# Unit 0's distance bias of two score groups moved into PSUM by TensorE, with a new order of the attention steps

## The chip, the core and the metric

The kernel runs on one core of a Trainium2 chip. The metric is device time in microseconds of one launch. Engines are named as in the profile: PE (TensorE, matmuls; PEld its weight loads), DVE (VectorE), ACT (ScalarE), POOL (GpSimd), SP (SyncE, which here only issues DMAs).

## The reference

Local attention with a few global keys, and behind it a mixture of experts whose tokens are dealt out evenly. Batch 4, 8 heads, 768 positions, head size 64, everything float32 at the interface:

```python
scores = scale * np.matmul(q, k.transpose(0, 1, 3, 2))
rel = pos[:, None] - pos[None, :]
is_global = pos[None, :] < int(n_global)                 # n_global = 8
is_local = (rel >= 0) & (rel < int(n_local))             # n_local = 96
keep = is_global | is_local
dist = np.where(is_global & ~is_local, float(n_local), np.abs(rel))
scores = scores + (-slopes[:, None, None] * dist)        # slopes[h] = 2 ** -(h + 1)
scores = np.where(keep, scores, -1e9)
a = np.exp(scores - max); a = a / (sum + 1e-9)
x = (a @ v) as rows of 512 = 8 heads x 64                # 3072 tokens
logits = x @ w_gate; each expert takes 384 tokens in order of the logits
out[mask] = np.maximum(x[mask] @ w1[e], 0) @ w2[e]       # 8 experts, 512 -> 1024 -> 512
```

## The kernel before

**Three stages.** The attention fills about the first 116 us, the routing goes to about 149 us, and the experts (matmuls in bf16) to the end.

**How the attention is tiled.** There are 8 units, 0 to 7; a unit is half a batch, four heads. A unit has two head pairs n = 2u and 2u+1, which the step names call a and b. Only keys near the diagonal and the 8 global keys count, so the positions are cut into 7 key tiles of 120, each against 216 queries. The 7 tiles form three score groups, 0 (tiles 0, 1), 1 (tiles 2, 3) and 2 (tiles 4 to 6). Each group fills 432 columns of one PSUM bank for each of the four heads: four banks in all, `ps0` (two banks, pair a) and `ps1` (two banks, pair b). Group 1 of unit 0 alone is put into four other banks, `po0`, `po1`, `t0`, `t1`, which the attention uses later for other things.

**The steps of a unit.** `KT` and `QT` (DVE, L291) transpose the raw keys and queries in blocks; `KB` and `KP` (ACT, L299), `KS` (POOL, L305 and L306) bring the keys into the tiles' layout; `QO` and `QP` (L318; ACT, for some steps of units 0 and 1 POOL or DVE) do so for the queries. A number behind the letters is the half of a head's 64 channels (0 or 1); for unit 0 the first part of a copy has a step of its own (`KP`, `QP`). Then, for each group g:

- `S0`, `S1`, `S2` (PE, L350): the scores of the group for all four heads, float32.
- `BIga`, `BIgb` (DVE, L368): reads the scores from PSUM and the distances `Dm` from SBUF, writes scores − 8·slope·distance to the tile `P` in SBUF. Two instructions a step, one a head. When both pairs are done the `ps` banks are free for the next group.
- `EXga`, `EXgb` (ACT, L375): exponential of `P` in place, with the factor 1/8.

Then `AV0` and `AV1` (PE, L408) multiply `P` by the values, `OT` (ACT, L415) brings the result out of PSUM, `M0` and `M1` (POOL, L384 to L391) add up the overlapping tiles, `SU` (PE, L425 and L429) makes the sums and the gate's logits, `LT` (DVE, L465), `GT` (POOL), `TK` and `TO` (PE and DVE, L507 and L526) finish the rows. `C0` to `C17` build constants, `WT` starts loads of expert weights.

**What sets the order.** One list of step names, `ORDER`, is written out by hand, and the program is issued in it; each engine takes its own steps in that order and waits at each for what it needs. Ahead of the list stand the loads of units 0 and 1, 64 matmuls on a constant that nothing reads (`warm`, L583), and the building of `Dm` on POOL (L228 to L245). One step, `FW` (L605), is 15 float32 matmuls, 30 passes on PE, whose result nothing reads; it stands between `S2:0` and `S0:1`.

Of the kernel before, what the change touches and what calls it, by code (L numbers as in the profile page):

```python
# [9 lines left out]
FP32 = mybir.dt.float32  # L10
# [21 lines left out]
NT = 7  # L32
QW = 216
# [11 lines left out]
def kernel(  # L45
# [25 lines left out]
    nc.vector.tensor_copy(out=ident_bf, in_=ident)  # L71
# [62 lines left out]
    @later  # L134
    def _():
        nc.gpsimd.memset(tri_bf, 1.0 / 128.0)
        nc.gpsimd.affine_select(out=tri_bf, in_=tri_bf, compare_op=ALU.is_ge, fill=0.0,
                                base=-1, pattern=[[1, 128]], channel_multiplier=-1)
# [83 lines left out]
    with ExitStack() as actx:  # L222
# [23 lines left out]

        natp = actx.enter_context(tc.tile_pool(name="natp", bufs=1))
# [88 lines left out]
        def scores(u, g, spare=False):  # L336
            kA, qTt = kAs[u % 2], qTs[u]
            if spare:
                ps = [ps_o.tile([128, 512], FP32, tag=f"po{i}", name=f"psx{i}_{u}") for i in range(2)]
                ps += [ps_t.tile([128, 512], FP32, tag=f"t{i - 2}", name=f"psx{i}_{u}") for i in (2, 3)]  # L340
                at = lambda a: ps[a]
            else:
                ps = [ps_s.tile([128, 2, 512], FP32, tag=f"ps{w_}", name=f"ps{w_}_{u}_{g}") for w_ in range(2)]
                at = lambda a: ps[a // 2][:, a % 2, :]
            for i in GROUPS[g]:
                _, o, w = POS[i]
                for gd in range(2):
                    for a in range(4):
# [3 lines left out]
                                         start=(gd == 0), stop=(gd == 1), skip_group_check=True)  # L352
# [20 lines left out]
        def expo(n, g):  # L373
            P = Ps[n][:, 2 * g : 2 * g + 2].rearrange("p i t w -> p (i t w)")
            nc.scalar.activation(P, P, AF.Exp, scale=0.125)  # L375

# [162 lines left out]
        def consts_(*which):  # L539
# [767 lines left out]
```

## Time and profile before

| | |
|---|---|
| time, median of 3 runs | 247.12 us (247.04 to 247.24) |
| profiled execution, its own time | 245.83 us |
| span of its records | 244.0 us |
| PE busy | 230.1 us (94%) |
| DVE busy | 145.1 us (59%) |
| ACT busy | 154.1 us (63%) |
| POOL busy | 158.2 us (65%) |

The busy shares are of the whole span, which has three stages of different kind. The page's 40 slices and the table by stretch below say more: in the attention all four engines are busy most of the time, in the experts PE alone. The times of rows are microseconds from the start of the span. The time of a row of merged instructions is from the start of the first to the end of the last.

### The profile page before, as it was taken

What the parts mean: (1) busy time and instruction counts of PE and PEld (TensorE: products, weight loads), DVE (VectorE), ACT (ScalarE), POOL (GpSimd) and SP (SyncE); (2) the same over time, 40 slices, a digit from 0 to 9 for tenths busy, and PEclk for the clock granted to TensorE, in tenths of its full rate; (3) what the DMA queues carried; (4) which work ended last, traced back from release to release, by engine and by line L of the source; (5) the groups of instructions that cost most, each with busy time, mean ns of one, the idle gap of its engine ahead of it and who ended that gap; (6) DMA issues with size and microseconds to landing.
All of it is one profiled execution on the core that took longest, in us unless ns stands there. A gap on an engine that the chain in (4) does not pass through costs nothing.

```text
span 244.0 us, 6976 instructions
## 1 busy us (share of the span) xinstructions
PE 230.1 (94%) x2769; PEld 166.8 (68%) x2769; DVE 145.1 (59%) x323; ACT 154.1 (63%) x298; POOL 158.2 (65%) x290
## 2 busy tenths in 40 slices
PE   8899999999999999999778888999999999999990
PEld 7888888787878788787667746755555565655540
DVE  2998999999999886746887881332051423131220
ACT  2788999999999989744789942423425060524420
POOL 6456977899998999989220017785178685761322
PEclk9999999999999999999999999999999999999998
DMA  6998999699963899999999334999999999999412
GB/s 254 345 368 147 270 377 212 189 293 185 246 125 72 156 203 182 204 166 181 217 212 251 132 131 84 197 168 184 280 257 162 264 209 241 251 149 294 139 48 93
DMA packets 51545, 49.65 MB, mean 203 GB/s; under 512 B 31024, under 2 KB 43056, under 8 KB 51504
## 3 DMA queue, kind: packets, MB, share of 16 engines
q0 software_dynamic: 15728, 26.22, 53.2%
q1 hardware_dynamic: 35776, 22.89, 36.0%
q8 instruction: 24, 0.39, 0.7%
q14 instruction: 17, 0.14, 0.2%
HBM read 56.05 MB, written 9.44 MB: 268 GB/s over the span
## 4 chain that ended last, share of the span: by engine, by line
PE 82%; DVE 7%; ACT 4%; DMA 3%; issue 1%; POOLq 0%; POOL 0%; DVEq 0%; ACTq 0%
PE po L1229 16%; PE po L408 16%; PE ps L350 16%; PE ph L1188 15%; PE t L425 5%; ACT x L522 4%; PE t L429 2%; DVE arena L291 2%; PE ph L1177 2%; PE pxe L1140 2%; DMA w_early<-in_k_dram 2%; PE psx L605 1%; PE pw L507 1%; DMA xe<-x_tok,idi 1%; PE t L507 1%
## 5 line engine op out<-in xcount | busy, mean ns | idle before, releaser
L1191 ACT ACTIVATE hT<-ph 128x384 bf16<-128x384 f32 x56 | 27.5, 491 | 47.5 <-PE ph L1188 46.9
L368 DVE SCALAR_TENSOR_TENSOR P<-Dm,ps 128x432 f32<-128x432 f32 x92 | 49.4, 598 | 12.1 <-PE ps L350 12.1
L375 ACT ACTIVATE P<-P 128x864 f32<-128x864 f32 x48 | 42.5, 928 | 4.6 <-DVE P L368 4.3
L408 PE MATMUL po<-P,v 128*64 128x216 f32 (+6 forms) x576 | 40.5, 293 | 0.0
L408 PEld LDWEIGHTS po<-P,v 128*64 128x64 f32 x576 | 34.1, 137 | 8.9 <-issue 3.1
L387 POOL TENSOR_TENSOR S<-P 128x576 f32<-128x576 f32 (+1 forms) x32 | 38.8, 1214 | 1.7 <-ACT P L375 1.6
L1098 POOL DMA_INDIRECT xe<-x_tok,idi x24 | 24.5, 1020 | 13.1 <-PE ph L1188 7.0
L291 DVE STREAM_TRANSPOSE arena<-w_early 128x768 f32<-128x768 f32 x32 | 29.6, 955 | 3.5 <-DMA w_early<-in_k_dram 3.5
L1229 PEld LDWEIGHTS <-hT 128*128 128x128 bf16 x192 | 18.3, 98 | 19.3
L299 ACT COPY kA<-arena 128x720 f32<-128x720 f32 (+2 forms) x18 | 24.0, 1348 | 5.5 <-DVE arena L291 5.5
L522 ACT ACTIVATE x<-pw,ri 128x64 bf16<-128x64 f32 x112 | 24.4, 346 | 2.8 <-PE pw L507 2.8
L1107 POOL DMA_INDIRECT out_dram<-w_early,ido x15 | 14.9, 994 | 14.7 <-DVE w_early L1232 8.7
L1232 DVE COPY w_early<-po 128x512 f32<-128x512 f32 x15 | 10.4, 691 | 20.3 <-PE po L1229 20.3
L350 PE MATMUL ps<-arena,kA 32*128 32x216 f32 (+2 forms) x416 | 20.9, 333 | 1.0 <-DVE arena L318 0.6
L350 PE MATMUL ps<-qT,kA 32*128 32x216 f32 (+2 forms) x448 | 21.9, 334 | 0.0
L1148 DVE COPY xT<-pxe 128x512 bf16<-128x512 bf16 x18 | 7.0, 417 | 21.9 <-PE pxe L1140 21.9
L415 ACT COPY oT<-po 128x384 f32<-128x384 f32 x32 | 15.1, 479 | 7.3 <-PE po L408 7.3
L350 PEld LDWEIGHTS ps<-qT,kA 32*128 32x128 f32 x448 | 18.7, 185 | 1.1 <-issue 0.3
L350 PEld LDWEIGHTS ps<-arena,kA 32*128 32x128 f32 x416 | 17.6, 185 | 2.7 <-POOL arena L318 1.1
L1229 PE MATMUL po<-w_late,hT 128*128 128x512 bf16 x72 | 16.5, 379 | 0.0
L1188 PE MATMUL ph<-xT,w_late 128*128 128x384 bf16 x96 | 16.1, 326 | 0.0
L1188 PEld LDWEIGHTS <-w_late 128*128 128x128 bf16 x96 | 9.4, 98 | 6.5
(199 smaller groups left out, 381.3 us busy)
## 6 DMA issues: line engine op xcount, KB each, us to landing
w_early<-in_k_dram SPq DMA_DIRECT2D x8, 768.0 KB
w_early<-in_q_dram SPq DMA_DIRECT2D x8, 768.0 KB
v<-in_v_dram SPq DMA_DIRECT2D x32, 180.0 KB
w_late<-in_moe_w_dram POOLq DMA_DIRECT2D x5, 1024.0 KB, 12.8
w_early<-in_moe_w_dram POOLq DMA_DIRECT2D x8, 512.0 KB, 9.0
w_last<-in_moe_w_dram POOLq DMA_DIRECT2D x4, 1024.0 KB, 11.2
arena<-in_moe_w_dram POOLq DMA_DIRECT2D x2, 1024.0 KB, 11.8
x_tok<-x SPq DMA_DIRECT2D x2, 768.0 KB
```

Source lines behind the costliest of these rows:

```text
L291: nc.vector.transpose(out=t, in_=raws[kind, u][:, :, 32 * g : 32 * g + 32])
L299: nc.scalar.copy(out=kAs[u % 2][:, g, i0:i1, 8:128].rearrange("p i (c j) -> p i c j", j=NJ), in_=t[:, i0 * NC5 : i1 * NC5, :].rearrange("p ...
L350: nc.tensor.matmul(at(a)[:, o : o + w], lhsT=kA[r, gd, i, :], rhs=qTt[r, gd, KT * i : KT * i + w], start=(gd == 0), stop=(gd == 1), skip_g ...
L368: nc.vector.scalar_tensor_tensor(out=Ps[n][:, 2 * g : 2 * g + 2, t, :], in0=W, scalar=-8.0 * slopes[2 * (n % NPAIR) + t], in1=st[:, 0 : 2 ...
L375: nc.scalar.activation(P, P, AF.Exp, scale=0.125)
L387: nc.gpsimd.tensor_tensor(out=to[:, :, :, 0:OV], in0=P[:, i0 : i0 + m, :, 0:OV], in1=P[:, i0 - 1 : i0 + m - 1, :, KT:QW], op=ALU.add)
L408: nc.tensor.matmul(po[n, bank][64 * t : 64 * t + 64, a - QB * bank : z - QB * bank], lhsT=v7[:, t, i, :], rhs=Ps[n][:, min(i, 5), t, a - q ...
L522: nc.scalar.activation(x[:, 2 * hf + i, 128 * jj + 64 * t : 128 * jj + 64 * t + 64], ps[:, i, 64 * t : 64 * t + 64], AF.Identity, scale=ri ...
L1098: tc.keep_in_program_order(nc.gpsimd.indirect_dma_start(out=xes[s], out_offset=None, in_=x_tok[:, :], in_offset=bass.IndirectOffsetOnAxis( ...
L1188: nc.tensor.matmul(ph, lhsT=w1_of(e)[:, kc, 128 * fc : 128 * fc + 128], rhs=xT_of[e][:, kc, :, :].rearrange("p t n -> p (t n)"), start=(kc ...
L1191: nc.scalar.activation(hT[:, fc, :], ph, AF.Relu)
L1229: pin(e, nc.tensor.matmul(po, lhsT=hT[:, t, fc, :] if e == 0 else hT[:, fc, 128 * t : 128 * t + 128], rhs=w2_of(e)[:, fc, :], start=(fc == ...
```

## The change

- The distances of two groups are also kept in bf16 (`Db`, an ACT copy of `Dm`), and four diagonal matrices `sid` with −8·slope on the diagonal are made (four DVE instructions). All these numbers are exact in bf16.
- New steps `PB1:0` and `PB0:0`: four bf16 matmuls each, `sid` times `Db`, 432 columns into each head's bank. The scores of groups 0 and 1 of unit 0 are then added on top of that. `BI0` and `BI1` of unit 0 (four steps, eight DVE instructions) fall away.
- The exponential of those groups reads PSUM and writes `P`: for group 0 one ACT instruction a pair, for group 1, whose heads lie in separate banks, two.
- `FW` is gone, and `warm` has 48 matmuls instead of 64.
- The copies of the queries of units 0 and 1 change engine: `QO0:0` and `QO0:1` from POOL to DVE, `QO1:0` from POOL to ACT, `QO1:1` from ACT to DVE, `QP0:0` from ACT to DVE, `QP1:0` from DVE to ACT.
- The cast of `ident_bf` goes from DVE at the start to POOL, in the constant step `C6`.
- The list `ORDER` is new for all units.

```diff
-    nc.vector.tensor_copy(out=ident_bf, in_=ident)
...
+        nc.gpsimd.tensor_copy(out=ident_bf, in_=ident)
         nc.gpsimd.memset(tri_bf, 1.0 / 128.0)
...
+        Db = wmp.tile([128, WB - W0A], BF16)
+        sid = wmp.tile([128, 4, 128], BF16)
+
+        def distances_bf():
+            for h in range(4):
+                nc.vector.tensor_scalar(out=sid[:, h, :], in0=ident, scalar1=-8.0 * slopes[h], scalar2=None, op0=ALU.mult)
+            nc.scalar.copy(out=Db, in_=Dm[:, W0A : WB])
...
+        biased = {}
+
+        def distance_bias(u, g):
+            ps, at = biased[u, g] = score_banks(u, g)
+            lo = (W0A, WA, WA)[g]
+            D = Db[:, WA:WB].rearrange("p (o w) -> p o w", o=1).to_broadcast([128, 2, QW]) if g == 1 else Db[:, lo : lo + 2 * QW]
+            for a in range(4):
+                nc.tensor.matmul(at(a)[:, 0 : 2 * QW], lhsT=sid[:, 4 * (u % 2) + a, :], rhs=D, start=True, stop=False, skip_group_check=True)
...
-                                         start=(gd == 0), stop=(gd == 1), skip_group_check=True)
+                                         start=(gd == 0 and (u, g) not in biased), stop=(gd == 1), skip_group_check=True)
...
         def expo(n, g):
+            u, w_ = divmod(n, 2)
+            if (u, g) in biased:
+                if g == 0:
+                    Ps[n] = pp.tile([128, NT - 1, 2, QW], FP32, tag="P", name=f"P{n}")
+                to = Ps[n][:, 2 * g : 2 * g + 2]
+                ps = pss[u, g]
+                if len(ps) == 4:
+                    for t in range(2):
+                        nc.scalar.activation(to[:, :, t, :], ps[2 * w_ + t][:, 0 : 2 * QW].rearrange("p (i w) -> p i w", w=QW),
+                                             AF.Exp, scale=0.125)
+                else:
+                    nc.scalar.activation(to.rearrange("p i t w -> p t i w"),
+                                         ps[w_][:, :, 0 : 2 * QW].rearrange("p t (i w) -> p t i w", w=QW), AF.Exp, scale=0.125)
+                return
...
-            "KT0:0 KT1:0 KB0:0 QT0:0 KP1:0 QT1:0 KP0:0 KS0:0 KS1:0 QP1:0 KT0:1 QP0:0 QO0:0 S0:0 KB1:0 QO1:0 KB0:1 "
+            "KT0:0 KB0:0 KS0:0 PB1:0 KT1:0 QT1:0 C12:0 KS1:0 PB0:0 QT0:0 KP1:0 QP0:0 KP0:0 QP1:0 KT1:1 KB1:0 "
...
-        QCOPY = {"QO0:0": nc.gpsimd.tensor_copy, "QO1:0": nc.gpsimd.tensor_copy, "QO0:1": nc.gpsimd.tensor_copy}
+        QCOPY = {"QO0:0": nc.vector.tensor_copy, "QO0:1": nc.vector.tensor_copy, "QO1:1": nc.vector.tensor_copy, "QP0:0": nc.vector.tensor_copy}
...
-            elif op == "FW":
-                for m in range(15):
-                    nc.tensor.matmul(pss[0, 1][2][:, 432:512], lhsT=ident, rhs=ident[:, 0:80],
-                                     start=True, stop=True, skip_group_check=True)
...
-            warm(64)
+            warm(48)
             distances()
+            distances_bf()
```

How instructions stand on DVE before, from the first transposes to unit 1's group 0 (`P_315` and `P_319` are the `P` tiles of pairs a and b of unit 0, `psx` the four other banks):

```order
L291 STREAM_TRANSPOSE arena<-w_early 128x768 x4
L71 CAST ident_bf<-ident 128x128
L318 COPY arena<-arena 128x336
L291 STREAM_TRANSPOSE arena<-w_early 128x768 x2
L368 SCALAR_TENSOR_TENSOR P_315<-Dm,ps_0_0_267 128x2x216 x2
L368 SCALAR_TENSOR_TENSOR P_319<-Dm,ps_0_0_268 128x2x216 x2
L291 STREAM_TRANSPOSE arena<-w_early 128x768 x2
L368 SCALAR_TENSOR_TENSOR P_319<-Dm,ps_0_2_332 128x2x216 x2
L368 SCALAR_TENSOR_TENSOR P_315<-Dm,ps_0_2_331 128x2x216 x2
L368 SCALAR_TENSOR_TENSOR P_315<-Dm,psx_0_293 128x2x216
L368 SCALAR_TENSOR_TENSOR P_315<-Dm,psx_0_294 128x2x216
```

The same place on DVE now (lines are those of the new text: L299 is the transpose, L326 the query copy, L387 the bias; here `P_319` is pair a):

```order
L299 STREAM_TRANSPOSE arena<-w_early 128x768 x4
L326 COPY arena<-arena 128x336
L299 STREAM_TRANSPOSE arena<-w_early 128x768
L326 COPY arena<-arena 128x432
L299 STREAM_TRANSPOSE arena<-w_early 128x768 x3
L326 COPY qT_331<-arena 128x768 x2
L387 SCALAR_TENSOR_TENSOR P_319<-Dm,ps_0_2_338 128x2x216 x2
L387 SCALAR_TENSOR_TENSOR P_315<-Dm,ps_0_2_339 128x2x216 x2
L299 STREAM_TRANSPOSE arena<-w_early 128x768 x2
L387 SCALAR_TENSOR_TENSOR P_425<-Dm,ps_1_0_385 128x2x216 x2
L387 SCALAR_TENSOR_TENSOR P_428<-Dm,ps_1_0_384 128x2x216 x2
```

Eight bias instructions of unit 0 are gone, four query copies stand there instead of one, and both transposes of unit 2 that follow stand ahead of unit 1's first bias.

On ACT before, from the first key copy to the first copy out of the values' product:

```order
L299 COPY kA_135<-arena 128x4x120
L299 COPY kA_135<-arena 128x2x120 x2
L318 COPY arena<-arena 128x336
L299 COPY kA_135<-arena 128x4x120
L299 COPY kA_136<-arena 128x6x120 x2
L375 ACTIVATE P_315<-P_315 128x864
L318 COPY qT_375<-arena 128x768
L375 ACTIVATE P_319<-P_319 128x864
L375 ACTIVATE P_315<-P_315 128x864 x2
L299 COPY kA_135<-arena 128x6x120
L415 COPY oT_447<-po_0_410 128x2x6x32
```

And now, without the two exponentials of the last pair's group 1 and what follows them (L307 is the key copy, L404 and L401 the exponential out of PSUM, L408 the one in place):

```order
L307 COPY kA_136<-arena 128x4x120
L307 COPY kA_136<-arena 128x2x120 x2
L326 COPY arena<-arena 128x336
L307 COPY kA_136<-arena 128x4x120
L326 COPY arena<-arena 128x432
L404 ACTIVATE P_315<-ps_0_0_255 128x2x2x216
L404 ACTIVATE P_319<-ps_0_0_254 128x2x2x216
L307 COPY kA_137<-arena 128x6x120
L401 ACTIVATE P_319<-psx_0_239 128x2x216
L401 ACTIVATE P_319<-psx_0_240 128x2x216
L307 COPY kA_137<-arena 128x6x120
L408 ACTIVATE P_319<-P_319 128x864
```

The two exponentials of group 0 stand ahead of both key copies of unit 1, and the 768-wide query copy is gone from here.

On PE before, behind unit 0's group 2 (`po_0` is the values' product of pair a):

```order
L350 MATMUL ps_0_2_332<-arena,kA_135 128x48 x2
L605 MATMUL psx_0_295<-ident 128x80 x15
L350 MATMUL ps_1_0_390<-qT_375,kA_136 128x216 x2
L350 MATMUL ps_1_0_391<-qT_375,kA_136 128x216 x2
```

And now (L369 the scores, L441 the values' product):

```order
L369 MATMUL ps_0_2_339<-arena,kA_136 128x48 x2
L441 MATMUL po_0_367<-P_319,v_0_138 64x216 x4
L441 MATMUL po_0_367<-P_319,v_0_138 64x144 x2
L441 MATMUL po_0_367<-P_319,v_0_138 64x24 x2
L369 MATMUL ps_1_0_384<-qT_331,kA_137 128x216 x2
L369 MATMUL ps_1_0_385<-qT_331,kA_137 128x216 x2
```

Where the 15 unread matmuls stood, pair a's first values' product now stands.

## Rows read from the trace of the kernel before

**Rows 1.** By stretch: us, busy (x instructions) by engine, granted clock, DMA share, GB/s
```profile
9.30:16.30 7.00, 5.98 (x114) 5.09 (x113) 6.65 (x9) 5.61 (x5) 2.12 (x6) 1.00 1.07 316
21.50:83.00 61.50, 61.47 (x1140) 51.22 (x1140) 58.12 (x107) 59.92 (x70) 55.95 (x127) 1.00 0.84 207
83.00:116.00 33.00, 32.73 (x588) 26.44 (x588) 22.50 (x50) 23.10 (x31) 30.99 (x61) 1.00 1.13 188
149.40:236.50 87.10, 87.10 (x560) 49.79 (x561) 23.20 (x46) 31.45 (x63) 51.62 (x53) 1.00 0.94 200
```

**Rows 2.** Chain that ended last, 14 to 30 us: start, us, engine, tile, line
```profile
14.35 1.95 PE ps L350 x38
16.30 3.50 PE psx L605 x30
19.80 1.67 PE ps L350 x32
21.48 2.44 PE po L408 x36
23.92 1.67 PE ps L350 x32
25.59 0.79 PE t L425 x16
...
26.70 1.21 PE po L408 x16
27.91 1.96 PE ps L350 x44
```

**Rows 3.** Timeline, 5 to 24 us: start, us, engine, line, operation, shapes, count
```profile
5.31 3.68 DVE L291 STREAM_TRANSPOSE arena<-w_early 128x768 f32<-128x768 f32 x4 [3.50 <-DMA w_early<-in_k_dram]
6.32 2.08 ACT L299 COPY kA<-arena 128x480 f32<-128x480 f32 x3 [4.23 <-DVE arena L291]
8.19 1.93 POOL L318 COPY arena<-arena 128x432 f32<-128x432 f32 x2 [0.49 <-DVE arena L291]
8.29 0.80 ACT L318 COPY arena<-arena 128x336 f32<-128x336 f32 x1
9.17 1.26 DVE L318 COPY arena<-arena 128x336 f32<-128x336 f32 x1
9.30 0.65 PE L350 MATMUL ps<-arena,kA 32*128 32x216 f32 x8
10.35 1.82 DVE L291 STREAM_TRANSPOSE arena<-w_early 128x768 f32<-128x768 f32 x2
16.34 2.15 DVE L368 SCALAR_TENSOR_TENSOR P<-Dm,ps 128x432 f32<-128x432 f32 x4 [0.39 <-PE ps L350]
20.49 1.48 ACT L299 COPY kA<-arena 128x720 f32<-128x720 f32 x1
21.51 2.15 DVE L368 SCALAR_TENSOR_TENSOR P<-Dm,ps 128x432 f32<-128x432 f32 x4 [1.11 <-PE ps L350]
```

**Rows 4.** Timeline around 61 us, DVE and POOL
```profile
61.12 1.42 POOL L387 TENSOR_TENSOR S<-P 128x576 f32<-128x576 f32 x1
61.39 1.29 DVE L142 TENSOR_SCALAR w_early<-w_early 128x192 int32<-128x192 int32 x1
```

**Rows 5.** Groups with shapes kept apart, 0 to 117 us: busy us, mean ns
```profile
L375 ACT ACTIVATE P<-P 128x864 f32<-128x864 f32 x48 | 42.5, 928 | 4.6 <-DVE P L368 4.3
L415 ACT COPY oT<-po 128x384 f32<-128x384 f32 x32 | 15.1, 479 | 7.3 <-PE po L408 7.3
L318 ACT COPY qT<-arena 128x768 f32<-128x768 f32 x7 | 11.1, 1584 | 0.1
L318 POOL COPY qT<-arena 128x768 f32<-128x768 f32 x1 | 1.5, 1537 | 2.6 <-DVE arena L291 2.6
L583 PE MATMUL warm<-ones_bf 128*128 128x192 bf16 x64 | 8.2, 310 | 1.2 <-POOL ones_bf L73 1.2
```

**Rows 6.** Timeline of PE in the routing: bf16 matmuls of 512 columns
```profile
141.44 1.69 PE L767 MATMUL pw<-w_early,ident_bf 128*128 128x512 bf16 x7
```

More of the change, by code (lines that the diff above doesn't have):

```diff
@@ L334, in weight_piece, with score_banks, scores @@
                 nc.gpsimd.dma_start(dst, s_)
-        def scores(u, g, spare=False):
-            kA, qTt = kAs[u % 2], qTs[u]
-            if spare:
+        def score_banks(u, g):
+            if (u, g) == (0, 1):
                 ps = [ps_o.tile([128, 512], FP32, tag=f"po{i}", name=f"psx{i}_{u}") for i in range(2)]
                 ps += [ps_t.tile([128, 512], FP32, tag=f"t{i - 2}", name=f"psx{i}_{u}") for i in (2, 3)]
[L341 to L344, printed above, removed]
+                return ps, lambda a: ps[a]
+            ps = [ps_s.tile([128, 2, 512], FP32, tag=f"ps{w_}", name=f"ps{w_}_{u}_{g}") for w_ in range(2)]
+            return ps, lambda a: ps[a // 2][:, a % 2, :]
+        biased = {}
[5 more added lines that the diff above has]
+                nc.tensor.matmul(at(a)[:, 0 : 2 * QW], lhsT=sid[:, 4 * (u % 2) + a, :], rhs=D, start=True, stop=False, skip_group_check=True)
+        def scores(u, g):
+            kA, qTt = kAs[u % 2], qTs[u]
+            ps, at = biased.get((u, g)) or score_banks(u, g)
             for i in GROUPS[g]:
@@ L588, in step @@
         def step(op, u):
+            o = f"{op}:{u}"
             if (op, u) in done or not 0 <= u < NU:
@@ L595, in step @@
                 g = int(op[1])
-                pss[u, g] = scores(u, g, spare=(u == 0 and g == 1))
+                pss[u, g] = scores(u, g)
+            elif k == "PB":
+                distance_bias(u, int(op[2]))
             elif k in ("KT", "QT"):
@@ L609, in step @@
             elif k == "QP":
-                qT_out(0, int(op[2]), 0, 14, nc.vector.tensor_copy if op == "QP1" else nc.scalar.copy)
+                qT_out(0, int(op[2]), 0, 14, copy=QCOPY.get(o, nc.scalar.copy))
             elif op == "WG":
@@ L621, in step @@
             elif k == "QO":
-                qT_out(u, int(op[2]), 0 if u else 14, copy=QCOPY.get(f"{op}:{u}", nc.scalar.copy))
+                qT_out(u, int(op[2]), 0 if u else 14, copy=QCOPY.get(o, nc.scalar.copy))
             elif k == "BI":
```

48 rows, old and new, of the table ORDER are left out of this document.

## The prediction

> **What bounds the kernel now.** I read the table by stretch first. From 21.5 to 83 us PE is busy 61.47 of 61.50 us, and from 149.4 to 236.5 us all of the time [rows 1]. So in the attention and in the experts every microsecond taken off PE's start arrives at the end, if nothing else falls behind. Next to PE stands ACT with 59.92 of 61.50 us in the first of these stretches: it must be let start earlier too, since it can hardly catch up. Only before 21.5 us is there room; there PE is busy 5.98 of 7.00 us [rows 1], and behind it come the 30 passes of `FW`, 3.50 us on the chain [rows 2].
>
> Then the chain of waits [rows 2]: it runs from `S2:0` (to 16.30) through `FW` to `S0:1` at 19.80 and from there along PE only. The reader is to see that `FW` stands on the chain although nobody reads it. How much it costs is not its length: `S0:1` needs the banks that unit 0's `BI2` frees, and these four instructions end at 16.34 + 2.15 = 18.49 [rows 3]. So `FW` holds PE up by 19.80 − 18.49 = 1.3 us there.
>
> Last the timeline of the start [rows 3], to lay the new order on its durations. The first scores begin at 9.30, and `S2:1` begins at 27.91 [rows 2]. Between these, PE does S0:0, S1:0, S0:1, S1:1 at 1.67 each, S2:0 at 1.89 (that is `S2:1`'s 1.96 less its small waits, an estimate), both values' products of pair a 2.44, `SUa` 26.70 − 25.59 = 1.11, and AV0b 1.21 [rows 2]: 13.3 of 18.6 us. The other 5.3 us are `FW` (3.5) and 1.8 of waits.
>
> **The change, step by step.** I lay each engine's new order down with the old durations; a step begins when its engine is free and its inputs are there, and 0.1 to 0.2 us pass from engine to engine.
>
> *DVE.* The first four transposes end at 8.99, as before [rows 3], 0.92 each. The price of a query copy on DVE is the unknown: the only one before took 1.26 us for 336 columns. But it ran from 9.17 to 10.43, and POOL's two copies from 8.19 to 10.12 [rows 3]: it ended 0.31 us after POOL. The same pattern stands at 61 us: a DVE instruction of 192 columns took 1.29 us and ended at 62.68, beside a POOL instruction that ended at 62.54 [rows 4]. So I read 0.31 us as the copy itself, 0.92 ns a column: 0.31, 0.40 and 0.71 us for 336, 432 and 768 columns. The far bounds for 768 columns are 1.54 us, POOL's own price [rows 5], and 1.26 × 768/336 = 2.9 us; from the other side, 0.35 us if half of the 0.31 was still waiting.
>
> [...] POOL no longer has query copies there, only short key copies and constants. [...]
>
> So DVE: `QP0:0` to 9.3, transpose 10.2, `QO0:0` 10.6, three transposes 13.4, `QO0:1` and `QO1:1` 14.8, then it waits for `S2:0`. The transposes of unit 1 ran at 10.35 before without waiting for their load [rows 3]; now the first stands at 9.3, so up to 1 us of wait is possible there, which the 0.5 us of slack at 14.8 takes up in part.
>
> *ACT.* `Db` and the four `sid` instructions lie ahead of 5.31, while DVE and ACT have no data [rows 3]. The first key copies take 6.32 to 8.40 [rows 3], `QP1:0` 0.80 to 9.2, the second 480-wide key copy half of 2.08, as 480 are half of that row's 960 columns, to 10.2, `QO1:0` 0.98 (between 0.80 for 336 and 1.58 for 768 columns [rows 3, 5]) to 11.2. The exponential out of PSUM is not in the trace. In place it takes 0.93 for 864 columns; a copy out of PSUM takes 0.48 for 384 [rows 5]. Scaled by columns that is 1.08, an upper bound, since part of the 0.48 is fixed; below, nothing excludes that it is cheaper than in place: a quarter less would bring 0.5 us over the first two. I take 0.93, the row with the same operation and width, and 2 × 0.52 for the split ones.
>
> *PE.* 48 warm matmuls at 8.16/64 = 0.128 us [rows 5] end at 7.3; the 8 new bf16 matmuls of 432 columns cost between 0.128 (192 columns) and 0.24 each (512 columns, 1.69/7 [rows 6]), so 1.0 to 1.9 us, and end by 9.3. That is before the scores can start, so they cost nothing; without this cover they would cost 1.9. The 16 warm matmuls less (2.0 us) gain nothing for the same reason. `S0:0` 9.4 to 11.1. `S1:0` waits for `QO1:0`, 11.3 to 12.9. `EX0b`, `EX0a` 11.3 to 13.2 free the banks, `S2:0` 13.3 to 15.2, one microsecond earlier than before.
>
> *On from there.* ACT: key copy (1.48 [rows 3], less the small overlap of instructions that follow each other) to 14.6, `EX1a` to 15.6, key copy to 17.1, `EX2a` 18.0, `EX1b` 19.0, `EX2b` 19.9, unit 2's key copy 21.4. PE: `AV0a` 15.7 to 16.9. DVE: `BI2a`, `BI2b` 15.4 to 17.5 (2.15 [rows 3]). PE: `S0:1` 17.5 to 19.2, `AV1a` to 20.4. DVE: two transposes of unit 2 to 19.4, `BI0` of unit 1 to 21.5. PE waits 1.1 us for it: `S1:1` 21.6 to 23.3, `AV0b` 24.5, `SUa` 25.6, `S2:1` at 25.7 instead of 27.91.
>
> **The sum.** 27.91 − 25.7 = 2.2 us. In the other direction: 5.3 us without work before (`FW` 3.5, waits 1.8) become 3.0 (waits at S1:0, S2:0, AV0a, S0:1, S1:1 and S2:1), and the start is 0.1 later. About 1 us of it is `FW` alone; the rest is that unit 0's first exponentials no longer wait for DVE. What is late next is DVE's `BI0` of unit 1, behind two transposes.
>
> Does it stay? At `S2:1` ACT has finished unit 2's key copy at 21.4, before at 20.49 + 1.48 = 21.97 [rows 3], but then it still had `EX0b` and `EX1b` to do, 1.86 us: it is 2.4 us ahead. DVE ends unit 1's `BI0` at 21.5 instead of 21.51 + 2.15 = 23.66 [rows 3], and POOL has three query copies less. So all four engines lead by 2.2 or more, and the same work follows. In the routing and the experts nothing is removed; loads there start from buffers and steps that move along.
>
> The profiled execution is 245.83 us with a span of 244.0. I forecast a span of 241.8 and 243.6 for a profiled execution; the median of the runs lies 1.29 above the profiled one, so 247.12 − 2.2 = 244.9 us. Its own range is 243.8 to 245.9: 1.1 better if DVE's transposes or `BI0` fall better than laid out, 1.0 worse with PSUM exponentials of 1.08 (0.4 in all) and the port waits (0.5).
>
> **Rivals.** *Slow query copies.* If a strided DVE copy costs POOL's price, 1.54 for 768 columns (0.67 and 0.86 for the others), DVE is through at 17.3 instead of 14.8, `BI2b` ends at 19.4, and all behind comes 1.9 later: gain 0.3, 246.8 us. For it: POOL and ACT both need some 2 ns a column in this access pattern [rows 5]. Against it: the 0.31. At 2.9 us it would be a loss of 3.7.
>
> *Given back later.* The new list moves steps in all units, PE has no free time from 21.5 to 83 and ACT 1.6 us [rows 1]. PE idled 33.00 − 32.73 = 0.27 us from 83 to 116 [rows 1]; such a wait in each of eight units would take back 2.2: 247.1. I expect less, 246.4 (a third of the gain left). For it: ACT's closeness. Against it: the 2.2 to 2.4 us of lead of each engine, and that the PE sequence of the units differs in few places.
>
> [...]
> [...]
>
> **Chances.** Forecast 0.63, slow copies 0.14, given back 0.12, clock 0.08, something else 0.03. A difference under 0.2% (0.5 us) can't be told from none here. Faster: 0.63, and of the others 0.04, 0.06 and 0.01, makes 0.74. Same: 0.05, 0.05 and 0.01, makes 0.11. Slower: 0.05 of the slow copies, 0.01 of the given back, the clock's 0.08 and 0.01, makes 0.15. The range that holds the time 8 times in 10 goes from 243.5 (the forecast's best and a little) to 247.1 (the two middle rivals).
>
> **What would show it.** Right: no idle PE above 1.3 us from 9 to 30 us; the first `S2:1` pass near 25.7; 768-wide DVE copies below 0.9 us; `EX0` of unit 0 near 0.93; PE busy all but 0.5 us from 21 to 81; granted clock 1.00; the first expert matmul 2.2 us earlier. Wrong: `S0:1` waiting for DVE copies beyond 18 us, waits of PE for ACT in units 2 to 5, a clock below 1.00 in the first 30 us, or a lead that is there at `S2:1` and gone at the routing.

## The result, and the profile after

The changed kernel takes 250.34 us (median of 4 runs, 249.99 to 250.64); the kernel before, beside it, 247.15. The ratio is 1.0129 with a 95% interval of 1.0111 to 1.0146: slower by 3.2 us, where 244.9 was forecast. The profiled execution took 250.55 us, its span is 248.8. Medians and ratios here and below are of undisturbed executions; the few that the chip ran slower are left out.

First the table by stretch of the changed kernel (PE, PEld, DVE, ACT, POOL busy with instructions, granted clock, DMA share, GB/s); it answers to [rows 1].
```profile
9.30:16.30 7.00, 6.27 (x128) 5.91 (x128) 6.96 (x10) 6.44 (x8) 3.74 (x10) 1.00 1.08 306
21.50:83.00 61.50, 58.76 (x1070) 48.75 (x1074) 53.48 (x98) 56.77 (x65) 49.24 (x113) 1.00 0.83 204
83.00:116.00 33.00, 31.68 (x570) 25.73 (x560) 22.60 (x50) 22.53 (x29) 29.53 (x56) 1.00 0.96 161
```
The clock is 1.00 in every stretch. The start is denser than before (6.27 against 5.98 us). But from 21.5 to 83 us, where PE had been idle for 0.03 us, it is now idle for 61.50 − 58.76 = 2.74 us, and for 1.32 instead of 0.27 us from there to 116. All four engines are less busy in the long stretch, so the loss lies in waits; the rows below show where.

Next the timeline of the start of the changed kernel, which answers to [rows 3] (start, us, engine, line, operation, shapes, count, idle time before it and what ended that).
```profile
9.09 0.45 DVE L326 COPY arena<-arena 128x336 f32<-128x336 f32 x1
9.69 1.74 PE L369 MATMUL ps<-arena,kA 32*128 32x216 f32 x32 [1.28 <-DVE arena L326]
10.35 0.55 DVE L326 COPY arena<-arena 128x432 f32<-128x432 f32 x1
11.51 1.67 ACT L404 ACTIVATE P<-ps 128x864 f32<-128x864 f32 x2 [0.56 <-PE ps L369]
13.23 1.96 PE L369 MATMUL ps<-arena,kA 32*128 32x216 f32 x48 [0.35 <-ACT P L404]
13.52 2.08 DVE L326 COPY qT<-arena 128x768 f32<-128x768 f32 x2
15.52 2.14 DVE L387 SCALAR_TENSOR_TENSOR P<-Dm,ps 128x432 f32<-128x432 f32 x4
17.80 1.73 PE L369 MATMUL ps<-qT,kA 32*128 32x216 f32 x28 [0.21 <-DVE P L387]
21.87 1.74 PE L369 MATMUL ps<-qT,kA 32*128 32x216 f32 x32 [0.98 <-DVE P L387]
25.99 1.96 PE L369 MATMUL ps<-qT,kA 32*128 32x216 f32 x48
```
L326 is the query copy, L404 the exponential out of PSUM, L387 the bias on DVE, and the five rows of PE are S0:0, S2:0, S0:1, S1:1 and S2:1. S2:1 begins at 25.99 instead of 27.91 [rows 2]: a lead of 1.92 us. So the start does what was forecast.

Then the same view where the lead goes, in unit 1's last and unit 2's first scores.
```profile
23.32 0.35 SPq L280 DMA_DIRECT2D w_early<-in_q_dram  x1
26.71 1.45 ACT L307 COPY kA<-arena 128x720 f32<-128x720 f32 x1
28.28 1.84 DVE L299 STREAM_TRANSPOSE arena<-w_early 128x768 f32<-128x768 f32 x2 [2.43 <-ACT kA L307]
30.04 2.11 DVE L387 SCALAR_TENSOR_TENSOR P<-Dm,ps 128x432 f32<-128x432 f32 x4
31.26 0.63 PE L369 MATMUL ps<-arena,kA 32*128 32x216 f32 x4 [0.87 <-DVE P L387]
32.29 1.73 PE L369 MATMUL ps<-arena,kA 32*128 32x216 f32 x28 [0.40 <-DVE P L387]
```
DVE stands still for 2.43 us ahead of unit 3's first transposes, `QT0:3` and `KT0:3`. Behind them in its queue is the bias `BI2` of unit 1, and S0:2 waits for that: 0.87 and 0.40 us. S0:2 ends at 34.02, in the kernel before at 32.24 + 1.74 = 33.98; the lead is gone. The row names ACT's key copy as what ended the idle time, but the first of the two transposes reads unit 3's query, whose load SP issued at 23.32 only. In the kernel before the same load and the first transposes of unit 3 stand so:
```profile
23.61 0.37 SPq L272 DMA_DIRECT2D w_early<-in_q_dram  x1
31.90 1.83 DVE L291 STREAM_TRANSPOSE arena<-w_early 128x768 f32<-128x768 f32 x2
32.24 1.74 PE L350 MATMUL ps<-arena,kA 32*128 32x216 f32 x32
36.71 0.92 DVE L291 STREAM_TRANSPOSE arena<-w_early 128x768 f32<-128x768 f32 x1
```
At 31.90 run the two key transposes, `KT0:3` and `KT1:3`. The query is read first by `QT1:3`, at 36.71. In the changed kernel DVE is ready for `QT0:3` at 28.28 − 2.43 = 25.85: the new list asks for the query 11 us earlier, and only 1.9 us of that is the lead.

Last, the waits of PE above 0.35 us from 40 us to the end of attention, with DVE's row beside the third.
```profile
45.63 0.44 PE L540 MATMUL t<-ident,oT 128*128 128x128 f32 x2 [0.56 <-DVE LT L498]
71.70 0.44 PE L540 MATMUL t<-ident,oT 128*128 128x128 f32 x2 [0.43 <-DVE LT L498]
88.94 2.17 DVE L122 TENSOR_SCALAR w_early<-w_early 128x128 int32<-128x128 int32 x1
93.56 2.16 PE L369 MATMUL ps<-arena,kA 32*128 32x216 f32 x48 [0.55 <-DVE P L387]
100.94 2.60 PE L441 MATMUL po<-P,v 128*64 128x216 f32 x35 [0.76 <-issue]
118.75 0.51 PE L462 MATMUL t<-oT,wgx 128*32 128x192 f32 x8
```
L540 is `TK`; the first two rows are of units 1 and 3. The idle time before 100.94 is marked "issue": PE waited for nothing that this row shows. Units 1 and 3 have `LTa` ahead of `TKa` in the new list: both use the same PSUM tile, so PE waits for DVE's transposes of it. L122 is `C4`, now between unit 6's biases. The last row is the last scoring work of unit 7: it ends at 119.26, before at 116.02. These 3.24 us are as much as the medians of the timed runs differ by (3.19). The two profiled executions differ by more, 250.55 − 245.83 = 4.72 us: the first expert matmul starts at 154.03 instead of 150.14, and the rest comes in the experts. The profiled execution of the kernel before lies 1.3 us under its own median; what makes the 1.5 us behind the attention is open.

### The profile page after: what moved, and what is told of

It is laid out like the page before. It is cut to its first block, busy times and chain, and to the rows that moved or that the text cites. A ratio compares the mean times of both kernels' runs of the same rounds, so it can differ in the third digit from the quotient of the medians.

```text
span 248.8 us, 6886 instructions
## 1 busy us (share of the span) xinstructions
PE 227.7 (92%) x2731; PEld 163.7 (66%) x2731; DVE 144.7 (58%) x321; ACT 153.6 (62%) x301; POOL 155.8 (63%) x288
## 4 chain that ended last, share of the span: by engine, by line
PE 70%; DVE 14%; ACT 6%; issue 4%; DMA 3%; POOLq 0%; POOL 0%; DVEq 0%; ACTq 0%
PE po L1262 16%; PE ph L1221 15%; PE ps L369 13%; PE po L441 12%; DVE P L387 5%; PE t L458 4%; ACT x L555 4%; DVE arena L299 3%; PE ph L1210 2%; PE pxe L1173 2%; DMA w_early<-in_k_dram 2%; PE t L462 2%; PE pw L540 1%; DMA xe<-x_tok,idi 1%; PE t L540 1%
## 5 line engine op out<-in xcount | busy, mean ns | idle before, releaser
L387 DVE SCALAR_TENSOR_TENSOR P<-Dm,ps 128x432 f32<-128x432 f32 x88 | 47.2, 598 | 12.3 <-PE ps L369 12.1
L408 ACT ACTIVATE P<-P 128x864 f32<-128x864 f32 x44 | 39.6, 936 | 5.7 <-DVE P L387 5.6
L441 PE MATMUL po<-P,v 128*64 128x216 f32 (+6 forms) x576 | 41.2, 293 | 0.8 <-issue 0.8
L441 PEld LDWEIGHTS po<-P,v 128*64 128x64 f32 x576 | 34.7, 137 | 9.4 <-issue 3.3
L299 DVE STREAM_TRANSPOSE arena<-w_early 128x768 f32<-128x768 f32 x32 | 29.3, 950 | 4.7 <-ACT kA L307 2.4
L307 ACT COPY kA<-arena 128x720 f32<-128x720 f32 (+2 forms) x18 | 24.2, 1358 | 0.9 <-DVE arena L299 0.9
L369 PE MATMUL ps<-qT,kA 32*128 32x216 f32 (+2 forms) x448 | 22.4, 334 | 1.8 <-DVE P L387 1.2
L369 PE MATMUL ps<-arena,kA 32*128 32x216 f32 (+2 forms) x416 | 20.9, 332 | 3.5 <-DVE P L387 1.8
L369 PEld LDWEIGHTS ps<-qT,kA 32*128 32x128 f32 x448 | 19.1, 185 | 4.0 <-issue 1.9
L369 PEld LDWEIGHTS ps<-arena,kA 32*128 32x128 f32 x416 | 17.9, 185 | 5.2 <-POOL XM L130 1.7
L458 PE MATMUL t<-S,onesx 128*32 128x192 f32 x256 | 14.3, 331 | 0.0
```

What stands on the lines that cost most here:

```text
L299: nc.vector.transpose(out=t, in_=raws[kind, u][:, :, 32 * g : 32 * g + 32])
L369: nc.tensor.matmul(at(a)[:, o : o + w], lhsT=kA[r, gd, i, :], rhs=qTt[r, gd, KT * i : KT * i + w], start=(gd == 0 and (u, g) not in biased ...
L387: nc.vector.scalar_tensor_tensor(out=Ps[n][:, 2 * g : 2 * g + 2, t, :], in0=W, scalar=-8.0 * slopes[2 * (n % NPAIR) + t], in1=st[:, 0 : 2 ...
L441: nc.tensor.matmul(po[n, bank][64 * t : 64 * t + 64, a - QB * bank : z - QB * bank], lhsT=v7[:, t, i, :], rhs=Ps[n][:, min(i, 5), t, a - q ...
L458: nc.tensor.matmul(pr[32 * gq : 32 * gq + 32, :], lhsT=onesx[:, t, :], rhs=S[:, t, 192 * gq : 192 * gq + 192], start=(t == 0), stop=True, ...
```

## The experiments

Theory A: the start gains its 1.9 us, and a few steps that the new list puts in bad places take back more. A1, for the place at 28.28: DVE waits for the load of unit 3's query. A2: it waits for ACT, as the row says. Theory C: the engines are so close to each other behind 21.5 us that any list loses the lead again.

**q3_first**: the load of unit 3's query is issued ahead of the second value pair's.
```
-        VLOAD = {"S0:0": 1, "S1:0": 2, "S2:0": 3}
+        VLOAD = {"S0:0": 1, "QT1:1": 2, "S2:0": 3}
```


> The changed kernel with one edit: the loads of pair 2's values are issued behind the step KT0:1, so that unit 3's query load stands ahead of them in SP's queue. Theory A (the transposes QT0:3, KT0:3 on DVE waited 2.43 us at 28.28 for that load, which was issued only at 23.3): that wait goes, DVE's first transposes of unit 3 start near 26, S0:2 ends near 32.2 instead of 34.0, and the kernel is 1.5 to 2 us faster than the changed one, near 248.6. Theory B (the wait is for ACT's key copy KB1:2, which the trace names and which ended at 28.16): the wait stays at 28.3 and the time at 250.3. Theory C (whatever is gained at the start is lost anyway, since ACT and DVE have no room): the wait goes, but the time stays near 250.3.

Measured 247.75 us against 246.42 for the kernel before on this chip, ratio 1.0046 (1.0014 to 1.0077). The timeline of this version:
```profile
17.57 1.30 SPq L280 DMA_DIRECT2D w_early<-in_q_dram  x1
26.66 1.45 ACT L307 COPY kA<-arena 128x720 f32<-128x720 f32 x1
26.92 1.84 DVE L299 STREAM_TRANSPOSE arena<-w_early 128x768 f32<-128x768 f32 x2 [1.12 <-POOL tri_bf L136]
29.37 2.51 PE L441 MATMUL po<-P,v 128*64 128x216 f32 x34 [0.56 <-DMA v<-in_v_dram]
```
DVE starts 1.36 us earlier, while ACT's key copy still runs: it wasn't ACT, and A2 falls. But 1.12 us of the wait are left, though the load was issued 9.4 us ahead, and PE now waits 0.56 us for a value load, one of those that were put back. Moving one load moved the wait.

**tk_first**: `LTa` of units 1 and 3 behind `TKa`.
```
-SUa:1 LTa:1 TKa:1 EX1b:2        -SUb:3 KB0:6 LTa:3 EX2a:4 TKa:3 S0:5
+SUa:1 TKa:1 LTa:1 EX1b:2        +SUb:3 KB0:6 EX2a:4 TKa:3 LTa:3 S0:5
```


> The changed kernel with one edit: the steps LTa:1 and LTa:3 stand behind TKa:1 and TKa:3 in the list, as in the kernel before, instead of ahead of them. Theory A (TK's matmuls write the PSUM tile that LT reads, so in the new list PE waits for DVE to have read it, at 45.2 and at 71.3): PE's waits of 0.56 and 0.43 us at L540 go, with the smaller ones around them 0.8 to 1.3 us in all, time near 249.3. Rival (PE waits there for what DVE and ACT owe it in any order): the waits move to the next S step and the time stays within 0.3 us of 250.3.

Measured 246.48 us, ratio 1.0009 (0.9974 to 1.0045): level with the kernel before beside it, where the changed kernel stood 3.2 us above. The wait at L540 is gone at both places, and with it the idle time at 100.94, which had not been expected. DVE's late start at unit 3 stays, and with it S0:2's wait of 0.61 us at 30.93.

**old_list_behind**: the new list up to the step ahead of `QT0:3`, and behind it the old list's remaining steps in their order.
```
-... EX1a:1 KB1:2 QT0:3 KT0:3 SUa:0 S2:1 EX0b:1 BI2a:1 ... (new list to its end)
+... EX1a:1 KB1:2 then all steps of the old list that haven't been done
```


> The changed kernel up to unit 1's group 1 (new bias by TensorE, new order, no FW), and from QT0:3 on the steps in the order of the list of the kernel before. Theory A (the new start is worth what the forecast said, and the loss lies in places of the new list behind 28 us): S2:1 starts near 26.0 as in the changed kernel, the lead of 1.9 us is kept, time 245.0 to 246.0 where before has 247.1. Theory C (ACT and DVE have no room behind, the lead can't be kept): S2:1 near 26.0, lead gone by unit 3, time 246.8 to 247.5.

Measured 244.62 us, ratio 0.9938 (0.9908 to 0.9967), and faster than both kernels. Its PE rows and DVE's at the place in question:
```profile
25.76 1.96 PE L369 MATMUL ps<-qT,kA 32*128 32x216 f32 x48
27.76 2.15 DVE L387 SCALAR_TENSOR_TENSOR P<-Dm,ps 128x432 f32<-128x432 f32 x4 [2.22 <-PE ps L369]
30.09 1.74 PE L369 MATMUL ps<-arena,kA 32*128 32x216 f32 x32
113.58 0.51 PE L462 MATMUL t<-oT,wgx 128*32 128x192 f32 x8
```
DVE idles here too, 2.22 us, but for PE's scores, with nothing queued behind a late load; S0:2 begins at 30.09 without a wait. With the same lead and the old places unit 3's transposes, keys at 29.82 and query at 34.49, wait for nothing. Attention ends 115.51 − 113.58 = 1.93 us earlier than before: the lead is kept to the end, and theory C falls.

**before_no_fw**: the kernel before without `FW`, all else the same.
```
-KS1:1 WG:0 S2:0 FW:0 QT1:1 QT0:1
+KS1:1 WG:0 S2:0 QT1:1 QT0:1
```


> The kernel before without the 15 unread matmuls FW, all else as it was. Forecast of the prediction: FW holds PE up by 1.3 us at S0:1, of which some 1 us reaches the end: 246.1. Rival (the array's clock falls behind the pause that FW filled): a granted clock under 1.00 between 17 and 30 us, and 247.5 or more. Second rival (given back later, by ACT): 247.1.

Measured 246.5 us, ratio 0.998 (0.9951 to 1.0008): no gain that can be told. The 0.4% that had been forecast lies in the interval too. The table by stretch of this version (PE, clock, DMA share, GB/s), and two of its rows, S2:0 and S0:1:
```profile
10.00:15.00 5.00, 4.44 (x60) 0.66 1.13 296
14.88 1.88 PE L350 MATMUL ps<-arena,kA 32*128 32x216 f32 x48
19.13 1.74 PE L350 MATMUL ps<-qT,kA 32*128 32x216 f32 x32 [2.37 <-DVE P L368]
```
S0:1 waits for DVE's `BI2` now and begins 0.6 us earlier than in the kernel before (19.13 instead of 19.73 in this view), though S2:0 stands 0.5 us later; attention ends 0.29 us earlier. So `FW` did hold PE up, but what its removal is worth at the end this run can't tell. The 0.5 us go with the clock: in the profiled execution it was 0.66 in the mean from 10 to 15 us, and S1:0 took 3.05 us from 12.03 on, where it took 1.67 us in the kernel before. From 5 to 10 us and from 15 us on the clock is 1.00. This isn't the rival of the expectation, which had the clock fall behind the pause that `FW` filled, between 17 and 30 us: the low stretch is over by 15 us, ahead of the place where `FW` stood (16.3), and through the pause itself the clock is 1.00. Just before it, or at its start, PE was idle for 1.00 us up to 9.29 and for 0.63 us up to 10.56; in the changed kernel it was idle for 1.28 us up to 9.69 and the clock stayed at 1.00. The mean clock of all 12 runs of this version lies at 0.980 to 0.989, against 0.986 to 0.998 for the kernel before on this chip. Why it is lower wasn't found.

On a second chip the changed kernel was run once more, and its bad places were mended one after the other. **after_again** is the changed kernel itself.

> The changed kernel unchanged, as the control on this chip for the three that follow. Both theories: 1.010 to 1.015 of the kernel before; SU of unit 7 ends near 119.3 us in its profile, the waits at 28.28 (DVE, 2.43), 45.6 and 71.7 (PE for LT, 0.56 and 0.43) and 100.9 (PE for v, 0.76) stand where they stood.

In the profile of this run the row of the late transposes itself names the load:
```profile
28.15 1.84 DVE L299 STREAM_TRANSPOSE arena<-w_early 128x768 f32<-128x768 f32 x2 [2.46 <-DMA w_early<-in_q_dram]
```
In the first profile of the changed kernel the semaphore that DVE waits for at this place got its last update from that load at 28.15, just ahead of the start at 28.28.

**keys_first**: unit 3's key transposes ahead of its query transposes.
```
-KB1:2 QT0:3 KT0:3 SUa:0 S2:1 ... AV0a:1 QT1:3 EX2a:1 KT1:3
+KB1:2 KT0:3 KT1:3 SUa:0 S2:1 ... AV0a:1 QT0:3 EX2a:1 QT1:3
```


> In the changed kernel the two key transposes of unit 3 change places with its two query transposes; no load is issued elsewhere in the list by hand. Theory A1 (DVE's 2.43 us before 28.28 are a wait for unit 3's query load, which is issued at 23.3 and shares the DMA engines with two units' values): the key load is there since long, DVE's transposes start near 25.8, BI2:1 starts at 27.8 by its scores, S0:2 near 30.5 instead of 31.26, and the end of attention is 0.8 to 1.9 us earlier: 247.9 to 249.5 us, ratio to before about 1.005. Theory A2 (the row's own releaser, ACT's copy of kA at L307, is what DVE waits for): the start stays at 28.2 and the time at 250.3. Theory C (any order of these steps behind the new start loses it again): the end stays at 119 whatever moves.

**keys_tk**: that and the edit of tk_first, word for word.

> As the last, and the two LTa (units 1 and 3) behind their TKa. Theory A (losses of separate placed waits add up): S0:3 near 43.6 to 44.2, no wait at L540; the two gains add: 3.1 from the one (as measured alone, 250.3 to 247.2) and 0.8 to 1.9 from the other: 245.3 to 246.6 us, ratio 0.995 to 0.999. Rival (the two waits hide each other: DVE, late at 28.28, is what makes LTa:1 late as well): no more than the 247.2 of tk_first.

**keys_tk_c4**: that and `C4:0` behind `KT1:7` instead of behind `TOa:4`.
```
-OT0b:4 KT1:7 EX0a:5 C13:0        -S1:6 TOa:4 C4:0 GTa:4
+OT0b:4 KT1:7 C4:0 EX0a:5 C13:0   +S1:6 TOa:4 GTa:4
```

> As the last, and C4 (two comparisons of DVE, 2.17 and 0.23 us beside POOL's tree in the changed kernel, 0.53 and 0.23 in the kernel before) moved up behind KT1:7 of the same list, close to the steps beside which it stood before. Theory A: L122 takes 0.5 to 0.6 us there, the wait of 0.55 to 0.67 at S2:6 goes, and 0.5 to 1.0 us with it: 244.5 to 245.8. Rival (L122 is long wherever POOL's tree runs, and that is nearly everywhere): about 2.2 us there as well, a wait at S2:5 in place of S2:6, and the time of keys_tk.

The measured times, the ratios to the kernel before on this chip, and the end of attention, which is the start of the last L462 row plus its 0.51 us (for the kernel before, from its first profile, taken on another chip):

| kernel | us | ratio, 95% | end of attention |
|---|---|---|---|
| before | 247.27 | 1 | 116.02 |
| after_again | 249.88 | 1.0101 (1.0078 to 1.0124) | 118.73 |
| keys_first | 248.32 | 1.0041 (1.0020 to 1.0062) | 116.98 |
| keys_tk | 246.13 | 0.9955 (0.9937 to 0.9973) | 114.77 |
| keys_tk_c4 | 245.80 | 0.9942 (0.9921 to 0.9964) | 114.06 |

At the end of attention the steps are 1.75, 2.21 and 0.71 us, 4.67 together. After_again lies 2.71 behind before, so with the three places mended attention ends 4.67 − 2.71 = 1.96 us ahead of before, and the lead at S2:1 was 1.92: the account closes. Of these 1.96 us, 247.27 − 245.80 = 1.47 reach the time. Now the rows. In keys_first:
```profile
25.78 1.83 DVE L299 STREAM_TRANSPOSE arena<-w_early 128x768 f32<-128x768 f32 x2
28.00 2.15 DVE L387 SCALAR_TENSOR_TENSOR P<-Dm,ps 128x432 f32<-128x432 f32 x4 [0.39 <-PE ps L369]
43.47 0.44 PE L540 MATMUL t<-ident,oT 128*128 128x128 f32 x2 [0.56 <-DVE LT L498]
98.66 2.60 PE L441 MATMUL po<-P,v 128*64 128x216 f32 x35 [0.82 <-issue]
```
With the keys first DVE starts at 25.78 without a wait: their load was there. That is A1, shown by two different edits and by the row of after_again. The waits at L540 and the idle time marked "issue" (here at 98.66) stay, until in keys_tk both are gone. All four profiles with `LTa` ahead of `TKa` behind the new start have this idle time, 0.49 to 0.82 us, and none of the four with `TKa` first has it. In the changed kernel the weight load next to it, at 101.04, names a value load (1.06 us); what PE stands idle for there is open. In keys_tk_c4:
```profile
78.48 2.34 POOL L342 DMA_DIRECT2D w_early<-in_moe_w_dram  x3
78.53 0.18 DVE L122 TENSOR_SCALAR w_early<-w_early 128x128 int32<-128x128 int32 x1
```
L122 takes 0.18 us here, less than the 0.5 to 0.6 expected, beside POOL that issues transfers, and PE's wait at S2:6 is gone. The end of attention moves by what was expected (0.71), the time by half of it (0.33, within the intervals). So the price of `C4` changes with what stands beside it on POOL, but by no simple rule: in the kernel before it took 0.53 us, also beside POOL issuing transfers.

The other way round: **before_placed** puts the two `LTa` and `C4` of the new list into the kernel before (`C17`, which must follow `C4`, moves too).
```
-EX1a:2 TKa:1 EX2a:2    -EX2a:4 TKa:3 M1b:3    -EX0a:5 C4:0 AV1b:4    -SUa:4 C17:0 SUb:4
+EX1a:2 LTa:1 TKa:1     +EX2a:4 LTa:3 TKa:3    +TOa:4 C4:0 OT0a:5     +KS1:7 C17:0 OT1b:5
```


> The kernel before with three places of the new list put into its own list and nothing else: LTa:1 straight ahead of TKa:1, LTa:3 straight ahead of TKa:3, and C4 (with C17, which must follow it) behind TOa:4, between unit 6's first two biases. Start, biases and query copies stay those of before. Theory A (these places cost what they cost in any list): PE waits of about 0.5 each ahead of TKa:1 and TKa:3, DVE's L122 grows from 0.53 to between 1.3 and 2.3, and the end of attention comes 1.0 to 2.0 us later than before's 116.0: ratio 1.004 to 1.008. Rival (they cost only in the changed kernel, whose POOL or DVE runs later): no waits at L507, ratio 0.998 to 1.002.

Measured 248.21 us against 246.55 on its chip, ratio 1.010 (1.0065 to 1.0134). The timeline:
```profile
45.11 0.44 PE L507 MATMUL t<-ident,oT 128*128 128x128 f32 x2 [0.50 <-DVE LT L465]
70.78 0.20 PEld L507 LDWEIGHTS t<-ident,oT 128*128 128x128 f32 x2 [1.07 <-DVE LT L465]
70.78 0.44 PE L507 MATMUL t<-ident,oT 128*128 128x128 f32 x2 [0.69 <-DMA v<-in_v_dram]
90.06 0.45 DVE L123 TENSOR_SCALAR w_early<-w_early 128x128 int32<-128x128 int32 x1
116.93 0.51 PE L429 MATMUL t<-oT,wgx 128*32 128x192 f32 x8
```
Both waits at `TK` (L507 here) are there, with the old start, and attention ends 1.42 us later: the price belongs to the place, not to the changed kernel. The matmul's row at 70.78 names a value load, but the weight load of the same matmul names DVE's `LT`. A third idle time, 0.51 us at 69.23 and again marked "issue", came with them. `C4` (L123 here) took 0.45 us only, so this part of the expectation failed: the place in the list doesn't fix what POOL does at that moment. The time grew by a little more than the end of attention; why is open.

**before_q3_first** does the same for the query transposes of unit 3.
```
-EX1b:1 KT0:3 AV1b:0 KT1:3 EX2a:1              -AV1b:1 QT0:3 OT0b:1 QT1:4
+EX1b:1 QT0:3 KT0:3 AV1b:0 QT1:3 KT1:3 EX2a:1  +AV1b:1 OT0b:1 QT1:4
```


> The kernel before with unit 3's query transposes ahead of its key transposes (QT0:3 before KT0:3, QT1:3 before KT1:3), as in the new list. Theory A1 (the changed kernel waits at 28.28 because it is 2 us ahead of a query load that is issued at the same 23.3 to 23.6 in both): before comes to this place at 27.69, the load lands near 28.2, so DVE waits about 0.5 and PE, whose next scores start at 32, little or nothing: ratio 0.999 to 1.003. Rival (this order of the transposes is bad by itself, at any time): the loss that it made in the changed kernel, 1.56 us: ratio 1.006.

In this list `QT1:4` overwrites unit 3's transposed query before `QO0:3` has read it, so one unit's scores are made of other numbers. Routing and experts then ran on these, and the 1301.94 us measured say nothing of the order; its attention can be read.
```profile
32.00 3.55 DVE L291 STREAM_TRANSPOSE arena<-w_early 128x768 f32<-128x768 f32 x4
37.73 1.73 PE L350 MATMUL ps<-arena,kA 32*128 32x216 f32 x28 [0.39 <-DVE P L368]
```
The expectation mistook the place: the two transposes near 27.7 are `KT1:2` and `QT0:2`, of unit 2. Unit 3's stand behind `BI2` of unit 1, at 32.00, and wait for nothing; the kernel before, which issues the load at 23.61, has its own there at 31.90. But now they are four in a row, the bias `BI0` of unit 2 behind them begins at 35.48 instead of 34.09, PE waits for it at S1:2, and attention ends 1.32 us later than in the kernel before (117.34). So this run doesn't bring the query to the place of the new list, ahead of `BI2:1`, and can't tell what that place costs without the lead. It shows another price: four transposes ahead of one bias, with no load late.

**old_behind_again** and **keys_tk_c4_again**: the two faster versions beside each other.

> The version old_list_behind once more, beside the next one on one chip: the new list up to unit 3's transposes, the old list's remaining steps behind it. 0.990 to 0.997 of the kernel before; the end of attention near 113.9.

> The version keys_tk_c4 once more, beside the last one on one chip: the new list with its three places mended. If the end of attention alone sets the time, the two are within 0.2%, since both ended it at 113.9. If the places of the loads behind it count as well (its first gathered x waits 0.63 us, the other's 1.14), they differ by up to 0.4%.

Measured 245.31 us, ratio 0.9936 (0.9912 to 0.9960), and 244.57 us, ratio 0.9923 (0.9899 to 0.9947). The intervals overlap: which is the better can't be told. In the profile of old_behind_again attention ends at 115.29, not near 113.9: PE stands idle for 1.07 us at 42.39, marked "issue", where the first profile of the same version has 0.34. So the lead isn't kept whole in every execution; this one took 247.16 us. Each beat the kernel before in both its timings, by 0.6 to 0.8%, and keys_tk_c4 beat the changed kernel beside it by 1 − 245.80/249.88 = 1.6%.

## Why the prediction was wrong

Right were these steps. The start: S0:0 at 9.69 (9.4 was forecast), S2:0 at 13.23 (13.3), S0:1 at 17.80 in its main part (17.5), S1:1 at 21.87 (21.6), S2:1 at 25.99 (25.7). The sum of 2.2 us measured 1.92 at that place. S2:0 came out right because two misses cancel: the scores began 0.3 late, and the first two exponentials took 1.67 us instead of 1.86. The exponential out of PSUM took 1.67/2 = 0.84 us a pass for 864 columns, within the bounds around 0.93. The two of 432 columns at 14.48 took 0.98 us together, 0.14 more than one of 864: part of the price doesn't go with the columns, as was assumed for the copy out of PSUM. From engine to engine 0.05 to 0.15 us passed at the places that set PE's start, where 0.1 to 0.2 was laid down: the exponentials end at 13.18 and S2:0 begins at 13.23, the query copy ends at 9.54 and S0:0 begins at 9.69. The granted clock was 1.00 in every stretch, as the sign for being right had it. The 0.08 that the chances give the clock was the author's estimate; in before_no_fw, which was to test it, the clock through that pause was 1.00. The 8 new matmuls, under way before the first scores, cost nothing.

One term was too small: the query copies on DVE. They took 0.45, 0.55 and 1.04 us for 336, 432 and 768 columns, where 0.31, 0.40 and 0.71 had been read out of a row that ended 0.31 us after POOL's. The two of 768 columns end at 15.60, 0.4 us after S2:0, and put `BI2` of unit 0 behind themselves: part of the 0.3 us by which S2:1 came later than forecast. POOL had nothing under way from 9.07 to 11.83 when the first two ran, so this is the copy's own price, 1.3 ns a column, and not a wait for POOL. The sign set for being right, under 0.9 us for 768 columns, failed here. In the range, 0.4 and 0.5 us were added up to 1.0; nothing hangs on it. The 0.5 us for "port waits" in it is a term that no run shows: the two copies of 768 columns took 2.08 us together with POOL at work from 13.38 to 14.89, 1.35 ns a column, against 1.34 and 1.27 for the first two with POOL idle, and no wait of a quarter of a microsecond a copy is to be seen. That about 1 us of the gain is `FW` alone stays open: before_no_fw can't tell it from none.

What failed is the paragraph "Does it stay?": all engines lead by 2.2 or more, it says, "and the same work follows". The work is the same, its order isn't. I had laid the new list down step by step only as far as S2:1 and called the rest alike; its one sentence on loads is on the routing and the experts, and the attention's loads are left out. Unit 3's query load is issued at nearly the same time in both kernels, 23.32 and 23.61. The old list first reads it at 36.71. The new list puts `QT0:3` ahead of `BI2:1`, and DVE, ready at 25.85, stands until 28.28. The lead is 1.9 of these 11 us, the rest is the list; and with the same lead and the old list nothing waits there. The late query cost 1.75 us. The new list holds three more places, which cost by the runs 2.9 us together: 2.21 for `TK` behind `LT` in two units, with the idle time marked "issue" that goes with it, and 0.71 for `C4`.

The rival "given back later" named the mechanism, but two things in it were wrong. It was capped at the lead of 2.2 us, as if a list could only give back what it had gained; here the bad places cost 4.7. And it was sought in small waits in each of eight units, where it was a few waits at single places: PE is idle for 2.74 us from 21.5 to 83, where "all but 0.5 us" was to be seen. Of the marks that the prediction set for being wrong the last one came: a lead that is there at S2:1 and gone at the routing.

## What to carry to other kernels

When a change comes with a new order, an estimate of the part that it is about is half of the work: walk the rest of the new list too, above all where two steps that share a tile or a queue have changed places, and ask of each such pair what the second one waits for. A new order moves the readers of a load, and a lead moves them too, while the load may stay where it was: write down when each load behind the gain is issued and landed, and which step reads it first now. And test a list in halves: new start with old rest told in one run that the idea was good and its list was not.

## What the hardware showed

The first instruction of `C4`, on DVE with 128 columns, took between 0.18 and 2.28 us in the seven profiles in which it was read: 0.18 (keys_tk_c4) and 0.53 (the kernel before) beside POOL issuing transfers, 0.45 in before_placed, 1.32 in keys_tk, 2.19 in keys_first, 2.28 in tk_first, and 2.17 in the changed kernel at 88.94, beside a run of POOL's short copies and sums. These 2.17 us went past the end of single POOL instructions: the rows of the changed kernel from 88.89 on are
```profile
88.89 0.25 POOL L422 COPY S<-P 128x96 f32<-128x96 f32 x1
89.12 0.38 POOL L424 TENSOR_TENSOR S<-P 128x96 f32<-128x96 f32 x1
89.46 0.99 POOL L420 TENSOR_TENSOR S<-P 128x384 f32<-128x384 f32 x1
90.41 0.25 POOL L422 COPY S<-P 128x96 f32<-128x96 f32 x1
90.64 0.38 POOL L424 TENSOR_TENSOR S<-P 128x96 f32<-128x96 f32 x1
```
five of them, back to back, and L122 ended at 91.11, 0.09 us after the last, while POOL went straight on with its next copies. What made it take so long, and why it ended there, is open. And the row that says what ended DVE's idle time before 28.28 named ACT's key copy, which ended at 28.16, where the cause was a transfer that landed at 28.15, 0.01 us earlier. A second profile of the same kernel, in after_again, named the transfer: where two things end so close together, the row of one profile can name the wrong one.
